# Attention with 192 queries per head: a third of the exponentials moved behind the transpose, with the shift on GpSimd and row sums on TensorE

## Chip, cores, metric

The kernel runs on one core of a Trainium2 chip. The metric is device time in microseconds (us), the median of several executions. Before: 1319.64 us (13 runs, 1319.27 to 1320.28). The record lists all runs named here as fast, that is, none lay more than 1.5% above the fastest of its kernel.

## The reference

```python
B, H, Sq, Sk, D = 16, 32, 192, 1024, 128          # bf16 inputs
def reference(q, k, v):
    scale = q.shape[-1] ** -0.5
    scores = jnp.einsum("bhqd,bhkd->bhqk", q, k) * scale
    p = softmax(scores, axis=-1)
    return jnp.einsum("bhqk,bhkd->bhqd", p, v)
```

## The kernel before

The 512 heads are handled in pairs. A pair has 2 x 192 query rows, which make three **units** of 128 rows: rows 0 to 127 of head a, the same of head b, and the remaining 64 + 64 rows together. So there are 768 units. Sixteen heads, 24 units, form a **group**; the buffers for K, Q and V hold two groups, and there are 32 groups. Per unit:

- TensorE: scores (128x1024), later eight transposes of the probabilities, later the product with V.
- VectorE: a pass that copies the scores out of PSUM, scaled by -1/sqrt(D), and takes the row minimum (which is minus the row maximum); after each third unit, the division by the row sum.
- ScalarE: the exponential, which also accumulates the row sum.
- VectorE and ScalarE by turns: the copy of the transposed probabilities out of PSUM.

```python
# parts of the kernel; "..." and waits not shown are cut
# TensorE
def qk(u):                       # scores; two PSUM buffers
    if u >= 2: pe.wait_ge(s_max, u - 1)
    ...
def tr(u):                       # eight 128x128 transposes
    pe.wait_ge(s_exp, u + 1)
    if u >= 2: wait_evac(u - 2)
    ...
for step in range(NU + 4):
    if step + 1 < NU:       qk(step + 1)
    if 0 <= step - 2 < NU:  tr(step - 2)
    if 0 <= step - 4 < NU:  pv(step - 4)
# VectorE
def rowmax(u):
    dve.tensor_scalar(ss[:, u % NSS, :], s_ps[u % 2][:], -scale, None, ALU.mult, ALU.min,
                      accum_out=nb[:, u % NSS: u % NSS + 1]).then_inc(s_max, 1)
def evac(u):                     # even u here, odd u on ScalarE
    dve.tensor_copy(pt_sb[:, u % NPT], pt_ps[u % 2][:]).then_inc(s_evd, 1)
# ScalarE
def exp(u):
    act.activation(p_sb[:, u % NP, :], ss[:, u % NSS, :], ACT_FN.Exp,
                   bias=nb[:, u % NSS: u % NSS + 1], scale=-1.0,
                   accum_out=rs[:, pr % NRS, O_SLOT[k3]: O_SLOT[k3] + 1]).then_inc(s_exp, 1)
# SyncE: one queue for everything
def loads(g):
    if g >= NS:                  # NS = 2 groups buffered
        e.wait_ge(s_qk, last_u + 1)
        e.wait_ge(s_pv, last_u + 1)
    e.dma_start_transpose(kt[:, s], kf[...])     # K, 4 MB
    e.dma_start_transpose(qt[:, s], qf[...])     # Q
    e.dma_start(vs[:, s], vf[...])               # V, 4 MB
for g in range(NGR):
    if g + NS < NGR: loads(g + NS)
    stores(g)                    # three DMAs, after s_on of the whole group
```

## Time and profile before

| what | value | read from |
|---|---|---|
| median time | 1319.64 us | the runs |
| period of 6 units | 10.01 us, every time | VectorE timeline |
| VectorE busy | 97% | profile page |
| ScalarE busy | 96% | profile page |
| transfers' share | 99.3% of 16 engines' span | queue table |
| instruction fetches | 132 packets | queue table, q8 |

These are lines of the profile page of the kernel before: busy time, the DMA queues (packets, MB, share), the chain that ended last, and groups of instructions (after the first bar: busy us and mean ns of one; after the second: idle time before them).

```profile
PE 1183.6 (90%) x16130; PEld 891.2 (68%) x16384; DVE 1272.9 (97%) x2432; ACT 1259.2 (96%) x1921; POOL 0.7 (0%) x6
...
q1 hardware_dynamic: 790528, 318.78, 99.3%
q8 instruction: 132, 2.16, 0.7%
...
DVE 45%; issue 32%; ACT 16%; PE 3%; SPq 1%; DMA 1%; DVEq 1%; ACTq 0%
...
L259 DVE TENSOR_SCALAR_CACHE_REDUCE ss<-s_ps 128x1024 f32<-128x1024 f32 x768 | 914.9, 1217 | 27.8 <-PE s_ps L175 23.3
L305 ACT ACTIVATE p_sb<-ss,nb 128x1024 bf16<-128x1024 f32 x768 | 877.4, 1144 | 29.9 <-DVE ss L259 21.3
...
L268 DVE COPY pt_sb<-pt_ps 128x1024 bf16<-128x1024 bf16 x384 | 263.4, 686 | 0.9 <-PE pt_ps L210 0.9
...
kt<-in_k_dram SPq DMA_TRANSPOSE x32, 19.4
```

The queue's 99.3% looks like a transfer limit, but the instructions show something else. The row maxima (L259) were idle before their start for 27.8 us in all, of which 23.3 are waits for scores, nearly all for the very first ones. The timeline of VectorE (start, duration, instruction) shows that it never stops:

```profile
603.08 1.22 DVE L259 TENSOR_SCALAR_CACHE_REDUCE ss<-s_ps 128x1024 f32<-128x1024 f32 x1
604.21 0.09 DVE L259 DVE_READ_ACCUMULATOR ss<-s_ps 128x1 f32 x1
604.21 0.17 DVE L277 RECIPROCAL rinv<-rs 128x3 f32<-128x3 f32 x1
604.42 0.56 DVE L279 TENSOR_TENSOR ob<-o_ps,rinv 128x384 bf16<-128x384 f32 x1
604.90 1.22 DVE L259 TENSOR_SCALAR_CACHE_REDUCE ss<-s_ps 128x1024 f32<-128x1024 f32 x1
606.03 0.08 DVE L259 DVE_READ_ACCUMULATOR ss<-s_ps 128x1 f32 x1
606.03 0.69 DVE L268 COPY pt_sb<-pt_ps 128x1024 bf16<-128x1024 bf16 x1
606.64 1.21 DVE L259 TENSOR_SCALAR_CACHE_REDUCE ss<-s_ps 128x1024 f32<-128x1024 f32 x1
```

Read the start-to-start distances: a row maximum holds VectorE 1.14 us, a copy 0.61, a reciprocal 0.21, a division 0.48. Six, three, two and two of them make the 10.0 us of a period. And in stretches of 2 us (columns: stretch, busy time of PE, PEld, DVE, ACT and POOL, granted clock, DMA share, GB/s) the transfers pause at the end of a group; this is one of the groups:

```profile
585.20:587.20 2.00, 1.76 (x22) 1.13 (x21) 2.00 (x4) 2.00 (x4) 0.00 (x0) 1.00 1.12 268
587.20:589.20 2.00, 2.00 (x38) 1.52 (x37) 2.00 (x5) 1.92 (x4) 0.00 (x0) 1.00 0.65 141
589.20:591.20 2.00, 1.75 (x25) 1.43 (x23) 1.97 (x4) 1.98 (x3) 0.00 (x0) 1.00 0.08 17
591.20:593.20 2.00, 1.74 (x30) 1.37 (x30) 2.00 (x6) 1.93 (x5) 0.00 (x0) 1.00 0.00 0
```

The DMA share adds up the times of all packets and comes to more than 1 here (1.12), so these times overlap, and 99.3% over a whole run is not "full". VectorE is the limit of the kernel before, and transfers have time to spare. How much, one group does not tell: the pause shown, 4.9 us between the last packet and the next, is the longest. Over 29 groups of this trace (all but those at start and end) it is 1.8 to 4.9 us, 3.3 on average, so a group's transfers took 36.7 us of its 40.

### The profile page before, as it was taken

To read this page: it belongs to the slowest core of one execution; us is meant where nothing else is said; L and a number is where in the kernel's file an instruction comes from. 1 tells how busy PE (TensorE), PEld (TensorE's weight loads), DVE (VectorE), ACT (ScalarE), POOL (GpSimd) and SP (SyncE) were. 2 spreads that over 40 slices of the span, in tenths; PEclk is the share of its full clock that TensorE was granted. 3 is DMA by queue.
4 is the path that set the end of the run, shared out by engine and by line. 5 is a ranking of instruction groups with operands and counts; after the bars stand their busy time and mean duration, and the time that the engine had idled before them with its cause. 6 is when DMAs were issued, how large, how long until landed. Compare 5 with 4: busy or idle time off the path is not lost.

```text
span 1317.6 us, 40501 instructions
## 1 busy us (share of the span) xinstructions
PE 1183.6 (90%) x16130; PEld 891.2 (68%) x16384; DVE 1272.9 (97%) x2432; ACT 1259.2 (96%) x1921; POOL 0.7 (0%) x6
## 2 busy tenths in 40 slices
PE   2999999999999999999999999999999999999997
PEld 1766767666776666767667676766767667676665
DVE  2899999999999999999999999999999999999997
ACT  2899999999999999999999999999999999999997
POOL 0000000000000000000000000000000000000000
PEclk9999999999999999999999999999999999999999
DMA  9989999999999999899999999999999999999961
GB/s 283 276 193 240 256 253 276 254 215 247 268 242 289 210 252 261 250 258 272 206 261 248 254 279 232 238 259 255 243 278 226 245 258 238 275 271 221 248 200 25
DMA packets 790714, 321.39 MB, mean 244 GB/s; under 512 B 724992, under 2 KB 724992, under 8 KB 790528
## 3 DMA queue, kind: packets, MB, share of 16 engines
q1 hardware_dynamic: 790528, 318.78, 99.3%
q8 instruction: 132, 2.16, 0.7%
q14 instruction: 54, 0.44, 0.1%
HBM read 134.22 MB, written 25.17 MB: 121 GB/s over the span
## 4 chain that ended last, share of the span: by engine, by line
DVE 45%; issue 32%; ACT 16%; PE 3%; SPq 1%; DMA 1%; DVEq 1%; ACTq 0%
DVE ss L259 33%; ACT p_sb L305 15%; DVE pt_sb L268 11%; PE pt_ps L210 1%; SPq L116 1%; DMA vs<-in_v_dram 1%; ACT pt_sb L315 1%; DVE rinv L277 1%; PE s_ps L175 1%; PE o_ps L233 0%; PE o_ps L231 0%; DVEq L258 0%; DVE ob L279 0%; PE s_ps L182 0%; SPq L119 0%
## 5 line engine op out<-in xcount | busy, mean ns | idle before, releaser
L259 DVE TENSOR_SCALAR_CACHE_REDUCE ss<-s_ps 128x1024 f32<-128x1024 f32 x768 | 914.9, 1217 | 27.8 <-PE s_ps L175 23.3
L305 ACT ACTIVATE p_sb<-ss,nb 128x1024 bf16<-128x1024 f32 x768 | 877.4, 1144 | 29.9 <-DVE ss L259 21.3
L210 PEld LDWEIGHTS pt_ps<-ident,p_sb 128*128 128x128 bf16 x6144 | 472.2, 148 | 256.5 <-issue 175.0
L210 PE MATMUL pt_ps<-ident,p_sb 128*128 128x128 bf16 x6144 | 523.6, 228 | 13.0 <-issue 1.3
L315 ACT ACTIVATE pt_sb<-pt_ps 128x1024 bf16<-128x1024 bf16 x384 | 390.9, 1018 | 20.6 <-PE pt_ps L210 9.6
L175 PE MATMUL s_ps<-kt,qt 128*128 128x512 bf16 x770 | 254.3, 386 | 108.6 <-DVE ss L259 59.4
L231 PE MATMUL o_ps<-vs,pt_sb 128*128 128x128 bf16 x4096 | 312.7, 219 | 4.4 <-DMA vs<-in_v_dram 4.4
L268 DVE COPY pt_sb<-pt_ps 128x1024 bf16<-128x1024 bf16 x384 | 263.4, 686 | 0.9 <-PE pt_ps L210 0.9
L231 PEld LDWEIGHTS o_ps<-vs,pt_sb 128*128 128x128 bf16 x4096 | 253.5, 99 | 4.6 <-DMA vs<-in_v_dram 4.6
L175 PEld LDWEIGHTS s_ps<-kt,qt 128*128 128x128 bf16 x1024 | 69.2, 98 | 138.7 <-DVE ss L259 116.8
L233 PE MATMUL o_ps<-vs,pt_sb 128*64 128x128 bf16 x2048 | 162.5, 222 | 0.2 <-ACT pt_sb L315 0.2
L237 PE MATMUL o_ps<-vs,pt_sb 128*64 128x128 bf16 x2048 | 162.5, 222 | 0.2 <-issue 0.2
L182 PE MATMUL s_ps<-kt,qt 128*64 128x512 bf16 x512 | 153.0, 380 | 0.9 <-DVE ss L259 0.5
L188 PE MATMUL s_ps<-kt,qt 128*64 128x512 bf16 x512 | 153.0, 380 | 0.0
L279 DVE TENSOR_TENSOR ob<-o_ps,rinv 128x384 bf16<-128x384 f32 x256 | 142.8, 558 | 8.7
L305 ACT ACTIVATION_READ_ACCUMULATOR p_sb<-ss,nb 128x1 f32 x768 | 145.7, 190 | 0.0
L233 PEld LDWEIGHTS o_ps<-vs,pt_sb 128*64 128x64 bf16 x2048 | 121.0, 109 | 17.8 <-ACT pt_sb L315 0.4
L237 PEld LDWEIGHTS o_ps<-vs,pt_sb 128*64 128x64 bf16 x2048 | 121.0, 109 | 0.0
L259 DVE DVE_READ_ACCUMULATOR ss<-s_ps 128x1 f32 x768 | 64.0, 83 | 0.0
L277 DVE RECIPROCAL rinv<-rs 128x3 f32<-128x3 f32 x256 | 43.3, 169 | 1.6 <-PE o_ps L237 1.6
L182 PEld LDWEIGHTS s_ps<-kt,qt 128*64 128x64 bf16 x512 | 40.7, 109 | 2.2 <-DVE ss L259 1.4
L188 PEld LDWEIGHTS s_ps<-kt,qt 128*64 128x64 bf16 x512 | 40.7, 109 | 0.0
(7 smaller groups left out, 2.2 us busy)
## 6 DMA issues: line engine op xcount, KB each, us to landing
vs<-in_v_dram SPq DMA_DIRECT2D x32, 4096.0 KB, 15.1
out_dram<-ob SPq DMA_DIRECT2D x32, 512.0 KB, 15.9
out_dram<-ob SPq DMA_DIRECT2D x64, 128.0 KB, 4.4
kt<-in_k_dram SPq DMA_TRANSPOSE x32, 19.4
qt<-in_q_dram SPq DMA_TRANSPOSE x32, 6.8
```

The costliest lines, as they stand in the source:

```text
L175: ins = pe.matmul(S[:, cs], qt[:, s, x * SQ: x * SQ + 128], kt[:, s, x * SK + 512 * c: x * SK + 512 * c + 512], start=True, stop=True,)
L182: pe.matmul(S[0:64, cs], qt[:, s, a * SQ + 128: a * SQ + 192], kt[:, s, a * SK + 512 * c: a * SK + 512 * c + 512], start=True, stop=True, ...
L188: ins = pe.matmul(S[64:128, cs], qt[:, s, b * SQ + 128: b * SQ + 192], kt[:, s, b * SK + 512 * c: b * SK + 512 * c + 512], start=True, sto ...
L210: ins = pe.transpose(PT[:, t, :], P[:, t: SK: KT_TILES], ident[:])
L231: ins = pe.matmul(O[:, O_SLOT[k3], :], PTS[:, t, :], vs[:, s, x, t, :], start=first, stop=last)
L233: pe.matmul(O[0:64, O_SLOT[k3], :], PTS[:, t, 0:64], vs[:, s, a, t, :], start=first, stop=last, tile_position=(0, 0),)
L237: ins = pe.matmul(O[64:128, O_SLOT[k3], :], PTS[:, t, 64:128], vs[:, s, b, t, :], start=first, stop=last, tile_position=(0, 64),)
L259: dve.tensor_scalar(ss[:, u % NSS, :], s_ps[u % 2][:], -scale, None, ALU.mult, ALU.min, accum_out=nb[:, u % NSS: u % NSS + 1],).then_inc(s ...
L268: dve.tensor_copy(pt_sb[:, u % NPT], pt_ps[u % 2][:]).then_inc(s_evd, 1)
L279: dve.tensor_tensor(ob[:, so, pg, 0:3, :], o_ps[pr % 2][:, 0:3, :], rinv[:, pr % 2, 0:3].unsqueeze(2).to_broadcast([128, 3, 128]), ALU.mul ...
L305: act.activation(p_sb[:, u % NP, :], ss[:, u % NSS, :], ACT_FN.Exp, bias=nb[:, u % NSS: u % NSS + 1], scale=-1.0, accum_out=rs[:, pr % NRS ...
L315: act.activation(pt_sb[:, u % NPT], pt_ps[u % 2][:], ACT_FN.Copy).then_inc(s_eva, 1)
```

## The change

The intent is to take the PSUM copies off VectorE without overloading ScalarE. Two units of six (route `R_W`) no longer compute the exponential before the transpose. GpSimd subtracts the row minimum (scores are then at most zero after the sign), TensorE transposes the shifted scores, and ScalarE applies the exponential while it empties PSUM: exponential and copy are one instruction. The row sum, which came free with the exponential, is now missing for these units, and TensorE makes it with eight one-column matmuls against ones. The other units keep the exponential in front (`R_EA`, `R_ED`); only one copy of six stays on VectorE. The lags between stages grow, with more buffers; and the K load no longer waits for the value matmuls of the old group.

```diff
+R_EA, R_ED, R_W = 0, 1, 2
+def _attention_kernel(..., LAGS=(2, 4, 5, 7), ROUTES=(R_W, R_EA, R_ED, R_W, R_EA, R_EA)):
 # SyncE, loads(g)
                 if g >= NS:
                     e.wait_ge(s_qk, last_u + 1)
-                    e.wait_ge(s_pv, last_u + 1)
                 e.dma_start_transpose(kt...); e.dma_start_transpose(qt...)
+                if g >= NS:
+                    e.wait_ge(s_pv, last_u + 1)
                 e.dma_start(vs...)
 # GpSimd
+            def shift(u):
+                gp.wait_ge(s_max, u + 1)
+                ...
+                gp.tensor_tensor(x_sb[:, u % NX, :], ss[:, u % NSS, :],
+                    nb[:, u % NSS: u % NSS + 1].to_broadcast([128, SK]), ALU.subtract).then_inc(s_xp, 1)
 # TensorE, pv(u)
+                if with_rs:      # route(u) == R_W; these are first units of a pair
+                    for t in range(KT_TILES):
+                        ins = pe.matmul(O[:, 3, sl: sl + 1], PTS[:, t, :], ones[:, 0:1],
+                                        start=False, stop=t == KT_TILES - 1, skip_group_check=True)
-            for step in range(NU + 4):      # tr two steps, pv four steps after the scores
+            for step in range(NU + L_PV):   # tr four, pv seven
 # VectorE, onorm: one reciprocal more per pair (sums from o_ps and from rs)
 # ScalarE
             def evac(u):
+                if route(u) == R_W:
+                    act.activation(pt_sb[:, u % NPT], pt_ps[u % 2][:], ACT_FN.Exp, scale=-1.0).then_inc(s_eva, 1)
+                else:
                     act.activation(pt_sb[:, u % NPT], pt_ps[u % 2][:], ACT_FN.Copy).then_inc(s_eva, 1)
 (cut: semaphores, counters, waits that follow the routes)
```

More of the change, by code (lines that the diff above doesn't have):

```diff
@@ L9, with _attention_kernel @@
 ALU = mybir.AluOpType
-def _attention_kernel(nc, q, k, v, out, G=16, NS=2):
+R_EA = 0
+R_ED = 1
+R_W = 2
+def _attention_kernel(nc, q, k, v, out, G=16, NS=2, LAGS=(2, 4, 5, 7), ROUTES=(R_W, R_EA, R_ED, R_W, R_EA, R_EA)):
     B, H, SQ, D = q.shape
@@ L21, in _attention_kernel @@
     NU = NGR * UPG
-    NPR = NGR * PPG
     KT_TILES = SK // 128
     scale = float(D) ** -0.5
-    NP = 3
-    NPT = 3
-    NSS = 3
+    L_X, L_TR, L_EV, L_PV = LAGS
+    assert 1 <= L_X < L_TR < L_EV < L_PV
+    NSS = L_X + 2
+    NX = L_TR - L_X + 2
+    NPT = L_PV - L_EV + 2
+    NSO = 2
     NRS = 4
-    NSO = 2
     qf = q.rearrange("b h s d -> (b h) s d")
@@ L35, in _attention_kernel, with route @@
     of = out.rearrange("b h s d -> (b h) s d")
-    def evac_on_dve(u):
-        return u % 2 == 0
-    evac_count = []
-    nd = na = 0
+    def route(u):
+        return ROUTES[u % len(ROUTES)]
+    x_cnt = []
+    ev_cnt = []
+    n_xa = n_xp = n_ea = n_ed = 0
     for u in range(NU):
-        if evac_on_dve(u):
-            nd += 1
-            evac_count.append(nd)
-        else:
-            na += 1
-            evac_count.append(na)
+        r = route(u)
+        if r == R_W:
+            n_xp += 1
+            x_cnt.append(n_xp)
+        else:
+            n_xa += 1
+            x_cnt.append(n_xa)
+        if r == R_ED:
+            n_ed += 1
+            ev_cnt.append(n_ed)
+        else:
+            n_ea += 1
+            ev_cnt.append(n_ea)
     with ExitStack() as es:
@@ L63, in _attention_kernel @@
         ob = sb("ob", [128, NSO, PPG, 4, 128], BF16)
-        p_sb = sb("p_sb", [128, NP, SK], BF16)
-        pt_sb = sb("pt_sb", [128, NPT, KT_TILES, 128], BF16)
         ss = sb("ss", [128, NSS, SK], F32)
         nb = sb("nb", [128, NSS], F32)
+        x_sb = sb("x_sb", [128, NX, SK], BF16)
+        pt_sb = sb("pt_sb", [128, NPT, KT_TILES, 128], BF16)
         rs = sb("rs", [128, NRS, 4], F32)
@@ L81, in _attention_kernel @@
         s_max = sem("s_max")
-        s_exp = sem("s_exp")
+        s_xa = sem("s_xa")
+        s_xp = sem("s_xp")
         s_tr = sem("s_tr")
+        s_eva = sem("s_eva")
         s_evd = sem("s_evd")
-        s_eva = sem("s_eva")
         s_pv = sem("s_pv")
@@ L105, in store_cnt, with wait_x, wait_evac @@
             return 48 * (g // NSO + 1)
+        def wait_x(eng, u):
+            if route(u) == R_W:
+                eng.wait_ge(s_xp, x_cnt[u])
+            else:
+                eng.wait_ge(s_xa, x_cnt[u])
+        def wait_evac(eng, u):
+            if route(u) == R_ED:
+                eng.wait_ge(s_evd, ev_cnt[u])
+            else:
+                eng.wait_ge(s_eva, ev_cnt[u])
         @block.sync
@@ L110, in loads @@
                 s = g % NS
+                last_u = (g - NS + 1) * UPG - 1
+                h0 = g * G
                 if g >= NS:
-                    last_u = (g - NS + 1) * UPG - 1
                     e.wait_ge(s_qk, last_u + 1)
-                    e.wait_ge(s_pv, last_u + 1)
-                h0 = g * G
                 e.dma_start_transpose(
@@ L155, in _ @@
             ).then_inc(s_setup, 1)
+            def shift(u):
+                gp.wait_ge(s_max, u + 1)
+                if u >= NX:
+                    gp.wait_ge(s_tr, u - NX + 1)
+                gp.tensor_tensor(
+                    x_sb[:, u % NX, :], ss[:, u % NSS, :],
+                    nb[:, u % NSS: u % NSS + 1].to_broadcast([128, SK]), ALU.subtract,
+                ).then_inc(s_xp, 1)
+            for u in range(NU):
+                if route(u) == R_W:
+                    shift(u)
         @block.tensor
@@ L194, in qk @@
                 ins.then_inc(s_qk, 1)
-            def wait_evac(u):
-                if evac_on_dve(u):
-                    pe.wait_ge(s_evd, evac_count[u])
-                else:
-                    pe.wait_ge(s_eva, evac_count[u])
             def tr(u):
-                pe.wait_ge(s_exp, u + 1)
+                wait_x(pe, u)
                 if u >= 2:
-                    wait_evac(u - 2)
-                P = p_sb[:, u % NP, :]
+                    wait_evac(pe, u - 2)
+                X = x_sb[:, u % NX, :]
                 PT = pt_ps[u % 2]
@@ L209, in tr @@
                 for t in range(KT_TILES):
-                    ins = pe.transpose(PT[:, t, :], P[:, t: SK: KT_TILES], ident[:])
+                    ins = pe.transpose(PT[:, t, :], X[:, t: SK: KT_TILES], ident[:])
                 ins.then_inc(s_tr, 1)
@@ L217, in pv @@
                     pe.wait_ge(svl[s], load_cnt(g))
-                wait_evac(u)
+                wait_evac(pe, u)
                 if k3 == 0 and pr >= 2:
@@ L222, in pv @@
                 PTS = pt_sb[:, u % NPT]
+                sl = O_SLOT[k3]
                 a = 2 * pg
@@ L225, in pv @@
                 ins = None
+                with_rs = route(u) == R_W
                 for t in range(KT_TILES):
@@ L230, in pv @@
                         x = a if k3 == 0 else b
-                        ins = pe.matmul(O[:, O_SLOT[k3], :], PTS[:, t, :], vs[:, s, x, t, :], start=first, stop=last)
-                    else:
-                        pe.matmul(
-                            O[0:64, O_SLOT[k3], :], PTS[:, t, 0:64], vs[:, s, a, t, :],
-                            start=first, stop=last, tile_position=(0, 0),
-                        )
-                        ins = pe.matmul(
-                            O[64:128, O_SLOT[k3], :], PTS[:, t, 64:128], vs[:, s, b, t, :],
-                            start=first, stop=last, tile_position=(0, 64),
-                        )
+                        ins = pe.matmul(O[:, sl, :], PTS[:, t, :], vs[:, s, x, t, :],
+                                        start=first, stop=last, skip_group_check=True)
+                    else:
+                        pe.matmul(O[0:64, sl, :], PTS[:, t, 0:64], vs[:, s, a, t, :],
+                                  start=first, stop=last, skip_group_check=True, tile_position=(0, 0))
+                        ins = pe.matmul(O[64:128, sl, :], PTS[:, t, 64:128], vs[:, s, b, t, :],
+                                        start=first, stop=last, skip_group_check=True, tile_position=(0, 64))
+                        if with_rs:
+                            pe.matmul(O[0:64, 3, sl: sl + 1], PTS[:, t, 0:64], ones[:, 0:1],
+                                      start=False, stop=last, skip_group_check=True, tile_position=(0, 0))
+                            ins = pe.matmul(O[64:128, 3, sl: sl + 1], PTS[:, t, 64:128], ones[:, 0:1],
+                                            start=False, stop=last, skip_group_check=True, tile_position=(0, 64))
+                if with_rs:
+                    for t in range(KT_TILES):
+                        ins = pe.matmul(O[:, 3, sl: sl + 1], PTS[:, t, :], ones[:, 0:1],
+                                        start=False, stop=t == KT_TILES - 1, skip_group_check=True)
                 ins.then_inc(s_pv, 1)
@@ L244, in _ @@
             qk(0)
-            for step in range(NU + 4):
+            for step in range(NU + L_PV):
                 if step + 1 < NU:
                     qk(step + 1)
-                if 0 <= step - 2 < NU:
-                    tr(step - 2)
-                if 0 <= step - 4 < NU:
-                    pv(step - 4)
+                if 0 <= step - L_TR < NU:
+                    tr(step - L_TR)
+                if 0 <= step - L_PV < NU:
+                    pv(step - L_PV)
         @block.vector
@@ L257, in rowmax @@
                 if u >= NSS:
-                    dve.wait_ge(s_exp, u - NSS + 1)
+                    wait_x(dve, u - NSS)
                 dve.tensor_scalar(
@@ L268, in evac @@
                 dve.tensor_copy(pt_sb[:, u % NPT], pt_ps[u % 2][:]).then_inc(s_evd, 1)
+            ri_total = [0]
             def onorm(pr):
@@ L276, in onorm @@
                     dve.wait_ge(sst[so], store_cnt(g - NSO))
-                dve.reciprocal(rinv[:, pr % 2, 0:3], rs[:, pr % NRS, 0:3]).then_inc(s_ri, 1)
-                dve.wait_ge(s_ri, pr + 1)
+                w_slots = sorted(O_SLOT[k3] for k3 in range(3) if route(3 * pr + k3) == R_W)
+                e_slots = sorted(O_SLOT[k3] for k3 in range(3) if route(3 * pr + k3) != R_W)
+                for slots, src in ((w_slots, o_ps[pr % 2][:, 3, :]), (e_slots, rs[:, pr % NRS, :])):
+                    if not slots:
+                        continue
+                    step_ = slots[1] - slots[0] if len(slots) > 1 else 1
+                    sel = slice(slots[0], slots[-1] + 1, step_)
+                    dve.reciprocal(rinv[:, pr % 2, sel], src[:, sel]).then_inc(s_ri, 1)
+                    ri_total[0] += 1
+                dve.wait_ge(s_ri, ri_total[0])
                 dve.tensor_tensor(
@@ L284, in onorm @@
                 ).then_inc(s_on, 1)
-            for step in range(NU + 8):
+            for step in range(NU + L_PV + 2):
                 if step < NU:
                     rowmax(step)
-                u = step - 3
-                if 0 <= u < NU and evac_on_dve(u):
+                u = step - L_EV
+                if 0 <= u < NU and route(u) == R_ED:
                     evac(u)
-                u = step - 5
+                u = step - L_PV - 1
                 if 0 <= u < NU and u % 3 == 2:
@@ L297, in _, with exp_first @@
         def _(act):
-            def exp(u):
+            def exp_first(u):
+                act.wait_ge(s_max, u + 1)
+                if u >= NX:
+                    act.wait_ge(s_tr, u - NX + 1)
                 pr, k3, g, pg = unit_info(u)
-                act.wait_ge(s_max, u + 1)
-                if u >= NP:
-                    act.wait_ge(s_tr, u - NP + 1)
-                if pr >= NRS and k3 == 0:
+                if pr >= NRS:
                     act.wait_ge(s_on, pr - NRS + 1)
                 act.activation(
-                    p_sb[:, u % NP, :], ss[:, u % NSS, :], ACT_FN.Exp,
+                    x_sb[:, u % NX, :], ss[:, u % NSS, :], ACT_FN.Exp,
                     bias=nb[:, u % NSS: u % NSS + 1], scale=-1.0,
                     accum_out=rs[:, pr % NRS, O_SLOT[k3]: O_SLOT[k3] + 1],
-                ).then_inc(s_exp, 1)
+                ).then_inc(s_xa, 1)
             def evac(u):
@@ L314, in evac @@
                     act.wait_ge(s_pv, u - NPT + 1)
-                act.activation(pt_sb[:, u % NPT], pt_ps[u % 2][:], ACT_FN.Copy).then_inc(s_eva, 1)
-            for step in range(NU + 4):
-                u = step - 3
-                if 0 <= u < NU and not evac_on_dve(u):
+                if route(u) == R_W:
+                    act.activation(pt_sb[:, u % NPT], pt_ps[u % 2][:], ACT_FN.Exp, scale=-1.0).then_inc(s_eva, 1)
+                else:
+                    act.activation(pt_sb[:, u % NPT], pt_ps[u % 2][:], ACT_FN.Copy).then_inc(s_eva, 1)
+            for step in range(NU + L_EV + 1):
+                u = step - L_EV
+                if 0 <= u < NU and route(u) != R_ED:
                     evac(u)
-                if 0 <= step - 1 < NU:
-                    exp(step - 1)
+                u = step - L_X
+                if 0 <= u < NU and route(u) != R_W:
+                    exp_first(u)
 def bass_standalone__mha_softmax__near_ridge_kernel(
```

## The prediction

> **What bounds the kernel now.** The steady state repeats every 6 units (one unit is one 128-row score tile) in 10.01 us, read from the timeline; 128 such periods are 1281 us of the 1317.6 us span, so start and end cost about 37 us. In the timeline VectorE has no gap: start to start, a row maximum (L259) holds it 1.14 us, a copy out of PSUM (L268) 0.61, a reciprocal 0.20, a normalisation 0.48. Six, three, two and two of them are 6.8+1.8+0.4+1.0 = 10.0 us. The page agrees: DVE 97% busy. ScalarE is close behind: exponential with its accumulator read 1.14 us, copy 0.91, so 6x1.14+3x0.91 = 9.5 us. TensorE's 90% is not its limit: where its timeline is dense a unit takes 0.43 (scores) + 0.49 (transposes) + 0.45 (values) = 1.37 us, 8.2 us per period. DMA is 99% in the queue table, but stretches of 2 us show it idle about 5 us of each 40 us group, where SyncE waits for TensorE; a group's transfers need about 35 us, or 8.8 us per period.
>
> **What the change moves, per 6 units.**
> - VectorE: two of three copies leave (-1.22 us); one more reciprocal per pair (2 x ~0.15, estimate from the 0.17 us reciprocal). About 9.1 us.
> - ScalarE: 4 exponentials with accumulator (4.55), 3 plain copies (2.72), 2 exponentials that empty PSUM without accumulator. I take those at 1.0 us: the 0.91 us copy plus about 0.09 for a bias operand (the Trainium skill, "ScalarE: Activation LUTs", What ACT_TABLE_LOAD costs, says each pointer operand adds about 93 ns; 1144 against 1018 ns here is compatible). About 9.3 us.
> - GpSimd: 2 subtractions of 128x1024 f32. No duration in this trace; the Trainium skill, "GPSIMD Engine Reference", Performance versus the Vector engine, gives 4497 ns for 2048 fp32 elements, so an estimate of about 2.3 us each, 4.6 us of 9.3. The transpose comes four steps after the scores, so this should be hidden.
> - TensorE: 16 one-column matmuls with full weight loads for row sums. Estimate 0.056 us each from the pace of the value matmuls, +0.9 us: 9.1 us.
> - DMA: same bytes. K loads are released earlier (they no longer wait for the value matmuls). The limit of about 8.8 us moves near, but stays below.
> - Deeper lags: about 4 us more at start and end.
>
> **On the critical path.** The whole 1.2 us of VectorE copies was on it, but three engines then stand at 9.1 to 9.3 us. ScalarE should bind; I add 0.1 us for waits between engines whose steps are uneven: 9.4 us. 128 x 9.4 + 41 = 1244 us.
>
> **Prediction: 1244 us, 8 in 10 between 1205 and 1290.** Faster by over 2%: 0.84; within 2%: 0.12; slower: 0.04.
>
> **What would show it.** Right: the period near 9.4 us; DVE and ACT both 96 to 99% busy; row maxima gapless or with small waits on the scores; L268 copies down from 384 to 128; GpSimd busy near 45%, seldom named as releaser; the chain of waits shared by ACT and DVE; DMA idle under 3 us per group. Wrong: GpSimd ops of 4 us or more with transposes waiting for them; row-sum matmuls at 0.1 us each, with VectorE waiting for TensorE; VectorE ops lengthened beside GpSimd; the value load waiting, or TensorE waiting for K.
>
> **What would make it wrong.** One-column matmuls costing twice the estimate would put TensorE at 10 us and cancel the gain. A DMA need closer to 37 us would make transfers the bound at 9.3 or above. If the exponential from PSUM costs no more than the copy, 1225 us is possible.

## The result, and the profile after

The kernel after takes 1251.97 us (median of 8 runs, 1249.52 to 1256.14), against 1319.64. Ratios in this document are the mean time of one kernel's fast runs over that of the other's of the same rounds, so they are not quite the ratio of the medians quoted. Here it is 0.9492 (95% interval 0.9479 to 0.9504). The prediction was 1244 us, and 1252 lies in its range. The runs now spread by 0.5%, before by 0.08%. The profiled run is not among the eight and is longer than each of them (1259.49 us, span 1257.8), so averages read from its trace are some 0.6% high.

From the profile page of the kernel after, the lines that answer to those shown of before:

```profile
PE 1174.3 (93%) x18179; PEld 956.4 (76%) x18432; DVE 1149.3 (91%) x2432; ACT 1180.3 (94%) x1665; POOL 486.0 (39%) x262
...
q1 hardware_dynamic: 790528, 318.78, 110.4%
q8 instruction: 148, 2.42, 0.8%
...
PE 88%; DMA 4%; issue 3%; ACT 3%; SPq 1%; DVE 0%; ACTq 0%; DVEq 0%
...
L301 DVE TENSOR_SCALAR_CACHE_REDUCE ss<-s_ps 128x1024 f32<-128x1024 f32 x768 | 910.6, 1220 | 87.9 <-PE s_ps L215 65.4
L188 POOL TENSOR_TENSOR x_sb<-ss,nb 128x1024 bf16<-128x1024 f32 x256 | 485.3, 1896 | 755.6 <-PE pt_ps L244 731.3
...
L370 ACT ACTIVATE pt_sb<-pt_ps 128x1024 bf16<-128x1024 bf16 x384 | 391.6, 1020 | 37.0 <-PE pt_ps L244 35.9
...
L368 ACT ACTIVATE pt_sb<-pt_ps 128x1024 bf16<-128x1024 bf16 x256 | 261.0, 1019 | 8.8 <-PE pt_ps L244 8.8
...
L310 DVE COPY pt_sb<-pt_ps 128x1024 bf16<-128x1024 bf16 x128 | 87.8, 686 | 1.8 <-PE pt_ps L244 1.8
...
kt<-in_k_dram SPq DMA_TRANSPOSE x32, 21.7
```

No engine is at 97% any more, and VectorE has 88 us of waits in front of its row maxima. Taking the start times of the row maxima from the trace, the distance of six units is 9.20 us in the median, but 9.54 on average; a group of 24 units takes 36.8 us when nothing is in the way, and up to 40.4. The first four groups after the start take 35.2 to 37.2 us, and from the ninth on the mean is 38.6. Before, a period was 10.01 us in the median and 10.04 on average.

So two things have to be explained: why the smooth period is 9.20, and what holds groups up. For the first, the timeline of ScalarE in a smooth stretch (accumulator reads left out):

```profile
599.76 1.16 ACT L357 ACTIVATE x_sb<-ss,nb 128x1024 bf16<-128x1024 f32 x1
...
600.90 1.16 ACT L357 ACTIVATE x_sb<-ss,nb 128x1024 bf16<-128x1024 f32 x1
...
602.03 1.03 ACT L368 ACTIVATE pt_sb<-pt_ps 128x1024 bf16<-128x1024 bf16 x1
603.07 1.02 ACT L370 ACTIVATE pt_sb<-pt_ps 128x1024 bf16<-128x1024 bf16 x1
603.99 1.14 ACT L357 ACTIVATE x_sb<-ss,nb 128x1024 bf16<-128x1024 f32 x1
```

An exponential in front still holds ScalarE 1.135 us, a copy 0.905. The exponential that empties PSUM (L368, 1019 ns) costs exactly what the copy (L370, 1020 ns) costs. Four and five of them are 9.07 us; only 0.13 us of a smooth period is slack, mostly at 602.03, where 1.04 us pass.

For the second, the timeline of SyncE's queue, start and time of each issue:

```profile
407.65 18.68 SPq L141 DMA_TRANSPOSE kt<-in_k_dram  x1
426.37 4.68 SPq L144 DMA_TRANSPOSE qt<-in_q_dram  x1
431.10 0.59 SPq L149 DMA_DIRECT2D vs<-in_v_dram  x1
...
445.74 0.72 SPq L164 DMA_DIRECT2D out_dram<-ob  x1
446.50 18.84 SPq L141 DMA_TRANSPOSE kt<-in_k_dram  x1
```

K of the next group is issued right after the last store: the pause of the kernel before is gone, and the queue goes round once in 38.5 us (eight rounds from 407.65 to 716.03). SyncE does not wait for the engines here: from the second such K load on, the scores that it has to wait for were done 11 to 18 us before its issue began. The engines could do a group in 36.8. In the first groups transfers are ahead and the difference is invisible; then the lead is used up, and TensorE starts to wait at group changes. The trace shows for what: in 23 of 30 group changes its first instruction for the new scores starts less than 0.15 us after K and Q, the later of the two, have landed. In the kernel before, K and Q had landed 6.7 to 9.2 us earlier than they were needed.

### The profile page after: what moved, and what is told of

It is laid out like the page before. It is cut to its first block, busy times and chain, and to the rows that moved or that the text cites. A ratio compares the mean times of both kernels' runs of the same rounds, so it can differ in the third digit from the quotient of the medians.

```text
span 1257.8 us, 44565 instructions
## 1 busy us (share of the span) xinstructions
PE 1174.3 (93%) x18179; PEld 956.4 (76%) x18432; DVE 1149.3 (91%) x2432; ACT 1180.3 (94%) x1665; POOL 486.0 (39%) x262
## 3 DMA queue, kind: packets, MB, share of 16 engines
q8 instruction: 148, 2.42, 0.8%
## 4 chain that ended last, share of the span: by engine, by line
PE 88%; DMA 4%; issue 3%; ACT 3%; SPq 1%; DVE 0%; ACTq 0%; DVEq 0%
PE pt_ps L244 32%; PE o_ps L267 18%; PE s_ps L215 16%; PE o_ps L270 11%; PE s_ps L222 8%; DMA vs<-in_v_dram 4%; PE o_ps L281 3%; SPq L141 1%; ACT x_sb L357 1%; ACT pt_sb L370 1%; ACT pt_sb L368 1%; PE o_ps L272 1%; SPq L144 0%; PE s_ps L228 0%; DVE ss L301 0%
## 5 line engine op out<-in xcount | busy, mean ns | idle before, releaser
L188 POOL TENSOR_TENSOR x_sb<-ss,nb 128x1024 bf16<-128x1024 f32 x256 | 485.3, 1896 | 755.6 <-PE pt_ps L244 731.3
L244 PEld LDWEIGHTS pt_ps<-ident,x_sb 128*128 128x128 bf16 x6144 | 480.4, 148 | 217.8 <-issue 143.0
L357 ACT ACTIVATE x_sb<-ss,nb 128x1024 bf16<-128x1024 f32 x512 | 584.9, 1148 | 23.1 <-DVE ss L301 23.1
L244 PE MATMUL pt_ps<-ident,x_sb 128*128 128x128 bf16 x6144 | 524.6, 229 | 1.2 <-ACT pt_sb L368 1.2
L370 ACT ACTIVATE pt_sb<-pt_ps 128x1024 bf16<-128x1024 bf16 x384 | 391.6, 1020 | 37.0 <-PE pt_ps L244 35.9
L368 ACT ACTIVATE pt_sb<-pt_ps 128x1024 bf16<-128x1024 bf16 x256 | 261.0, 1019 | 8.8 <-PE pt_ps L244 8.8
L357 ACT ACTIVATION_READ_ACCUMULATOR x_sb<-ss,nb 128x1 f32 x512 | 101.9, 199 | 0.0
L310 DVE COPY pt_sb<-pt_ps 128x1024 bf16<-128x1024 bf16 x128 | 87.8, 686 | 1.8 <-PE pt_ps L244 1.8
L281 PE MATMUL o_ps<-ones,pt_sb 128*128 128x1 bf16 x2048 | 87.5, 164 | 0.0
L281 PEld LDWEIGHTS o_ps<-ones,pt_sb 128*128 128x128 bf16 x2048 | 78.2, 96 | 0.0
```

The costliest lines, as they stand in the source:

```text
L188: gp.tensor_tensor(x_sb[:, u % NX, :], ss[:, u % NSS, :], nb[:, u % NSS: u % NSS + 1].to_broadcast([128, SK]), ALU.subtract,).then_inc(s_x ...
L244: ins = pe.transpose(PT[:, t, :], X[:, t: SK: KT_TILES], ident[:])
L281: ins = pe.matmul(O[:, 3, sl: sl + 1], PTS[:, t, :], ones[:, 0:1], start=False, stop=t == KT_TILES - 1, skip_group_check=True)
L357: act.activation(x_sb[:, u % NX, :], ss[:, u % NSS, :], ACT_FN.Exp, bias=nb[:, u % NSS: u % NSS + 1], scale=-1.0, accum_out=rs[:, pr % NRS ...
L368: act.activation(pt_sb[:, u % NPT], pt_ps[u % 2][:], ACT_FN.Exp, scale=-1.0).then_inc(s_eva, 1)
L370: act.activation(pt_sb[:, u % NPT], pt_ps[u % 2][:], ACT_FN.Copy).then_inc(s_eva, 1)
```

## The experiments

The theory, A: the engines alone would run at 9.20 us a period, and the transfers, at 38.5 us a group, set the time. The rival, B: the engines hold each other up at group changes, whatever the transfers do. A leads to a second question, because I had counted only 35 us of transfers in a group: where do the other 3.5 us come from?

### a1_no_v and b1_no_v: V loaded only twice

Wrong, with the same instructions on the compute engines.

```diff
-                if g >= NS:
-                    e.wait_ge(s_pv, last_u + 1)
-                e.dma_start(vs[:, s], ...).then_inc(svl[s], 16)
+                if g < NS:
+                    e.dma_start(vs[:, s], ...).then_inc(svl[s], 16)
-                    pe.wait_ge(svl[s], load_cnt(g))
+                    pe.wait_ge(svl[s], 16)
```

> The kernel after, with V loaded for the first two groups only (the output is wrong on purpose; instructions and waits of the engines are the same). Theory A (the engines alone would repeat every 9.20 us, and the transfers, at about 38.5 us a group, hold groups back): all periods 9.20 us, 22.7 + 127.8 x 9.20 + 16 = about 1215 us. Rival B (the engines hold each other up at group changes, whatever the transfers do): stays at 1250 us.

> The kernel before with the same cut (wrong output on purpose). Its transfers were said to fit in the 40 us of a group: unchanged, 1318 to 1320 us. If transfers cost the kernel before anything, it falls below 1315.

Measured: 1216.17 us for the kernel after without V (1214.7 to 1217.85; ratio to the kernel before 0.922), 1319.5 us for the kernel before without V. Nearly all groups of a1 take 36.7 to 36.9 us. So transfers cost the kernel after 36 us and the kernel before nothing. A holds, B falls. The granted clock is 0.998 instead of 0.988, but that looks like a result of the waits, not a rival cause: the trace of the kernel after grants half the clock for 3.4 us (once 6.8) at seven group changes, each at the end of a group of 39.2 us or more, after TensorE had waited; the trace of a1 does so only at its end.

### d1_dma_only: the transfers alone

```diff
-    (all work of TensorE, VectorE, ScalarE; the subtraction on GpSimd)
 # loads(g), for g >= NS
-                    e.wait_ge(s_qk, last_u + 1)
+                    e.wait_ge(sxk[s], load_cnt(g - NS)); e.wait_ge(sxq[s], load_cnt(g - NS))
-                    e.wait_ge(s_pv, last_u + 1)
+                    e.wait_ge(svl[s], load_cnt(g - NS))
 # stores(g): the output tile is set to zero once
-                e.wait_ge(s_on, (g + 1) * PPG)
+                e.wait_ge(s_setup, 3)
```

> The same loads and stores in the same order from the same queue, without the compute (the output is zeros, wrong on purpose). Theory A in its plain form (the DMA engines need about 38 us a group whatever else runs): 32 x 38 = about 1220 us. If the transfers alone need only the 35 us a group that I predicted: about 1120 us; then it is their order and waits, not their volume, that holds the kernel after. Far below 1100: transfers are slowed by the compute beside them.

Measured: 1067.94 us. The transfers by themselves go round in 33.2 us. So the plain form of A is wrong: the volume does not need 38.5 us; something slows the transfers while the engines work.

The trace of the kernel after names a suspect. In the stretch from 612 to 616 us, cut into 40 slices of 0.1 us, the K transposes run at 290 GB/s, then stop for about 1.2 us, in a stretch in which one packet of another queue, q8 (instructions), ran:

```profile
DMA  9999999999999900000000000089999999999999
GB/s 287 300 289 287 294 289 289 289 289 435 271 271 269 161 0 0 0 0 5 8 8 10 10 8 10 13 182 289 289 287 289 292 287 289 292 289 294 294 289 289
...
q8 instruction: 1, 0.02, 1.5%
```

These packets are the engines' own program. The Trainium skill, "Runtime: NRT & Kernel Launch", Instruction fetch mechanics, says that an engine's instruction memory is refilled in blocks of 16 KiB by a DMA queue that the sequencer drives. This trace agrees: 148 packets make 2.42 MB, 16.4 KB each, and the 44,565 instructions of the kernel after are mostly TensorE's. I counted the packets of the transposes in the 4 us after each of the 75 fetches that met them at full speed: in the median, packets worth 1.4 us are missing. That gives theory C: each instruction fetch halts the transposing transfers for about 1.4 us. Its rival, D: transfers are slowed by the compute engines' use of the on-chip memory, whatever is fetched.

### d2_dma_fetch and d3_dma_traffic: one suspect each

```diff
 # d2: d1 plus
+            for i in range(18200):      # one weight load and one matmul each, constant data
+                pe.matmul(o_ps[0][:, 0:2, 0:80], ones[:], ob[:, 0, 0, 0:2, 0:80], start=True, stop=True)
 # d3: d1 plus, each with two output buffers and its semaphore
+            for i in range(260):  gp.tensor_tensor(x_sb[...], ss[:, 2, :], nb[...], ALU.subtract)
+            for i in range(980):  dve.tensor_scalar(ss[:, i % 2, :], s_ps[0][:], -scale, ..., accum_out=...)
+            for i in range(980):  act.activation(x_sb[:, i % 2, :], ss[:, 3, :], ACT_FN.Exp, ..., accum_out=...)
```

> The transfers alone, beside a TensorE that only runs 18,200 idle matmuls (as many instructions as the kernel after gives it, on constant data, output zeros and wrong on purpose). Theory C (each 16 KB fetch of instructions holds the transposing transfers up for about 1.4 us; some 145 fetches): 1068 + 145 x (1.0 to 1.6) = 1210 to 1300 us by the stalls if every one hits a transpose, about 1180 us if half do. Rival D (the transfers are slowed by the compute engines' use of the on-chip memory): 1068 to 1080 us, as this TensorE reads next to nothing.

> The transfers alone, beside VectorE, ScalarE and GpSimd running the tile operations of the kernel after (980 row maxima, 980 exponentials, 260 subtractions of 128x1024, on constant data), with a tenth of the instructions. Theory C: 1068 plus about 18 fetches x 1.4 = 1070 to 1095 us. Rival D: near 1200 us.

Measured: 1271.92 us and 1135.7 us. I had set both expectations for the whole time, and that was a mistake of design: in both runs the added engine work lasts longer than the transfers (TensorE is busy 99% of d2, VectorE 99% of d3), so the total says nothing. The transfers must be read by themselves. These are the issues of K for the fourth and the last group in SyncE's queue, for d1, d2 and d3:

```profile
92.28 15.18 SPq L142 DMA_TRANSPOSE kt<-in_k_dram  x1
...
1022.96 15.27 SPq L142 DMA_TRANSPOSE kt<-in_k_dram  x1
```

```profile
103.80 17.95 SPq L142 DMA_TRANSPOSE kt<-in_k_dram  x1
...
1142.11 16.93 SPq L142 DMA_TRANSPOSE kt<-in_k_dram  x1
```

```profile
94.59 15.04 SPq L142 DMA_TRANSPOSE kt<-in_k_dram  x1
...
1027.67 15.31 SPq L142 DMA_TRANSPOSE kt<-in_k_dram  x1
```

Over 28 groups, that is 33.2 us a group alone, 37.1 beside 142 fetches of instructions, and 33.3 beside full VectorE, ScalarE and (for the first 40% of the run) GpSimd work with few instructions. (The page of d3 shows no q8 packets; its 4,445 instructions came with 34 packets of 8 KB on another instruction queue, q14.) C holds, and D falls for the engines of d3. In d2 TensorE's use of the memory grew together with its fetches, and no run separates the two, but the traces do. Between stalls the transfers are as fast in all of them: the median slice of 0.1 us that has packets of 256 bytes (transposes and stores) has 112 of them in d1, d2, d3 and the kernel after alike. Stalls of such packets of 1 to 3 us, with full speed before and after, number none in d1, one in d3, 62 in d2 and 67 in the kernel after; a q8 packet runs in, or within 1.5 us before, 58 of those 62 and all 67.

The remaining 1.4 us between 37.1 and the 38.5 of the kernel after were not settled by a run. Fetches come more often there (148 in 1257.8 us are 4.5 in a round; 142 in 1270.1 us are 4.1 in one of d2), and the q14 queue has 53 packets against 2 in d2; transposes pause beside some of these too, mostly for less than 1 us (near 609.4 us, for about 0.4).

### a2_wait_back: the old place of the wait

```diff
                     e.wait_ge(s_qk, last_u + 1)
+                    e.wait_ge(s_pv, last_u + 1)
                 e.dma_start_transpose(kt...)
 ...
-                if g >= NS:
-                    e.wait_ge(s_pv, last_u + 1)
                 e.dma_start(vs...)
```

> The kernel after with the wait for the value matmuls put back in front of the K load, as the kernel before has it. If transfers are the limit and the earlier start of K matters: slower than 1252, by up to 11 us a group where they are late (seven units of lag x 1.55 us), at most 1400 us. If SyncE reaches that wait only after it has been met, because its queue runs late by itself: unchanged within 5 us.

Measured: 1254.47 us (1252.7 to 1256.54; ratio to before 0.9507, interval 0.9493 to 0.9521, which overlaps that of the kernel after). This part of the change is worth nothing that can be measured here: SyncE's queue is late by itself.

### r2_old_routes and r3_no_gpsimd: one part of the change alone

```diff
-ROUTES=(R_W, R_EA, R_ED, R_W, R_EA, R_EA)
+ROUTES=(R_ED, R_EA)                                   # r2: split as before, long lags kept
+ROUTES=(R_EA, R_EA, R_ED, R_EA, R_EA, R_EA)           # r3: copies moved, no GpSimd
```

> The kernel after with its longer lags and earlier K loads, but the work split as in the kernel before (copies out of PSUM by turns on VectorE and ScalarE, no GpSimd, no row-sum matmuls). Theory: the gain is the moved work alone, so VectorE is full again at 10.0 us a period: 128 x 10.0 + 41 = about 1321 us. If lags or the earlier loads carried part of the gain: below 1310.

> The kernel after with copies moved off VectorE, but every exponential at ScalarE before the transpose (no GpSimd, no row sums). ScalarE then has six exponentials with accumulator and five copies: 6 x 1.135 + 5 x 0.905 = 11.3 us a period, 128 x 11.3 + 41 = about 1490 us, much slower than before: unloading VectorE alone is a loss.

Measured: 1315.43 us and 1486.84 us. In r2 the period is 10.01 us again. It is 4 us faster than the kernel before: its first group takes 37.4 us instead of 44.0, and the time after the last row maximum grows from 12.1 to 14.5. All but these 4 us of the gain need the moved work. In r3 the period is 11.34 us with ScalarE busy 98%: emptying VectorE alone makes the kernel 12.7% slower (ratio 1.1269). The fused exponential is what pays for the copies that come to ScalarE.

### r1_one_rowsum: fewer instructions in the real kernel

Wrong: one of eight row-sum matmuls is left.

```diff
-                    for t in range(KT_TILES):
-                        ins = pe.matmul(O[:, 3, sl: sl + 1], PTS[:, t, :], ones[:, 0:1], ...)
+                    ins = pe.matmul(O[:, 3, sl: sl + 1], PTS[:, 0, :], ones[:, 0:1], ...)
```

> The kernel after with one of the eight row-sum matmuls left per block (wrong output on purpose). 1,792 matmuls and as many weight loads less, 229 KB of instructions, 14 fetches of 16 KB. Theory C (fetches hold the transposes up, and transfers set the time): 14 x 1.4 = about 20 us less, 1228 to 1240 us. If transfers set the time but fetches do not matter: unchanged within 5 us. If TensorE's time mattered, the smooth period would fall below 9.20 us; I expect it to stay.

Measured: 1230.2 us (1228.6 to 1231.61), with 134 fetches instead of 148. From the ninth group on, a group takes 37.5 us instead of 38.6. The time fits theory C, but the run does not isolate it, because the smooth period fell too, against my expectation, from 9.20 to 9.09 us. That is close to the 9.07 us of ScalarE's own work. So in smooth stretches the row-sum matmuls on TensorE had cost 0.1 us a period beyond ScalarE's limit.

### p1_v_pool, p2_v_act and p3_v_pool_late: V on a queue of its own

The load of V does not have to stand in the queue of the transposes and stores.

```diff
 # SyncE: V for the first two groups only
-                if g >= NS:
-                    e.wait_ge(s_pv, last_u + 1)
-                e.dma_start(vs...)
+                if g < NS:
+                    e.dma_start(vs...)
 # GpSimd (p1, p3), after the subtraction of unit u; in p2 the same on ScalarE, at the start of step u
+            def load_v(u):
+                g = u // UPG + 1
+                if u % UPG != 9 or not NS <= g < NGR:      # p3: 15 instead of 9
+                    return
+                gp.wait_ge(s_pv, (g - NS + 1) * UPG)
+                gp.dma_start(vs[:, g % NS], vf[...]).then_inc(svp[g % NS], 16)
 (cut: TensorE waits for V on svp from the third group on; p2 keeps the semaphore svl)
```

> The kernel after with the V loads (from the third group on) issued by GpSimd on a queue of its own, once the group two before is through, so that they can run beside the transposes of K and Q. If the transfer engines as a whole are the limit (no free time in them): 1250 us, unchanged. If the limit is one queue that stands still during a stall of the transposes, V fills the holes: towards the 1216 us of the run without V, 1216 to 1235. If GpSimd's issue of a load takes over 4 us, row blocks will wait for its subtractions and it gets slower.

> The same, issued by ScalarE. ScalarE sets the 9.20 us period, so its issue (0.59 us on SyncE) is paid in full: 36.8 + 0.6 = 37.4 us a group, 1235 us, if V then no longer waits; 1250 us or more if the transfer engines as a whole are the limit.

> As p1_v_pool, but V is issued six units (9 us) later in a group, when the transposes of K and Q should have landed. If the two groups of p1 that lost 9 and 11 us lost them because V ran beside the transposes: all groups 36.8 us, 1216 to 1222 us. If they lost them for another reason: near 1235 again. If V now comes too late: value matmuls wait for it, over 1240.

Measured: p1 1234.95 us (1230.15 to 1241.69), p2 1298.52 us (1293.53 to 1300.36), p3 1219.83 us (1217.75 to 1220.67; ratio to before 0.9243). All three are correct. In p1 most groups take 36.7 us, but two take 46.0 and 47.5; around these, the issue of Q lasts 20.6 and 15.5 us instead of 4: V got in among the transposes. The trace shows how: the two queues take turns, about one packet each. From 85 to 90 us of p1, 75 to 95 packets of Q (256 bytes each) go through in a microsecond beside about as many of V (4 KB each), where 1,134 packets of the transposes go through without V (77 to 78 us). In the other 28 groups V ran almost only beside the stores, and K and Q had landed 9 us or more before they were needed. p2 has the same trouble in most groups, and my expectation for it was wrong by 60 us: the issue on ScalarE took only 0.38 us, but the loads of K and Q landed late. Their lines in the page of p2:

```profile
kt<-in_k_dram SPq DMA_TRANSPOSE x32, 29.3
qt<-in_q_dram SPq DMA_TRANSPOSE x32, 18.8
```

p3 starts V six units later and is the version that beats both kernels. SyncE's queue in p3 has its pause back in 18 of 30 groups, mostly about 5 us between the last store and the next K (V is under way then):

```profile
426.81 23.81 SPq L142 DMA_TRANSPOSE kt<-in_k_dram  x1
450.66 4.12 SPq L145 DMA_TRANSPOSE qt<-in_q_dram  x1
...
458.30 0.63 SPq L164 DMA_DIRECT2D out_dram<-ob  x1
463.61 23.75 SPq L142 DMA_TRANSPOSE kt<-in_k_dram  x1
```

Groups take 36.9 us on average (36.8 in most), and the time is 4 us above the run without V. The fetches are as many as before (148): p3 does not remove the stalls. It takes V out of the line behind them, and K and Q land over 1.2 us before they are needed in every group. V now runs beside the stores (the two small ones take 14.5 us to land instead of 4.4), and the issue of the next K lasts longer, 23.8 us instead of 18.7. How much of this comes from V using the stalls, and how much from V running beside the stores, was not separated.

## Why the prediction was right, and where it was wrong

The time was right to 8 us, but two errors of opposite sign stand behind that, so its closeness was partly luck: a smooth period of 9.20 instead of 9.4 us takes 26 us off 128 periods, and the transfers, which were not to matter, put 36 us back.

- **VectorE was the limit, and its copies were on the critical path**: right. Copies fell from 384 to 128, the period from 10.01 to 9.20 us; r2 and r3 show that the moved work, and only together with the fused exponential, makes the gain (all but some 4 us of it).
- **"ScalarE should bind", at 9.3 us a period**: in smooth stretches nearly so; its own work is 9.07. The term that was mis-sized is the exponential that empties PSUM: 0.905 us like the copy, not 1.0. I had allowed 0.09 us for a bias operand; the call in the kernel names none, and 1019 against 1020 ns shows no extra cost.
- **VectorE at 9.1 us**: about 8.9. The second reciprocal starts 0.08 us after the first (601.09 and 601.17 in the trace) and adds about 0.06 us, not 0.15.
- **GpSimd at 2.3 us a subtraction, hidden**: 1.90 us, and hidden. 731 of the 756 us that GpSimd was idle went on waiting for a buffer that a transpose frees.
- **TensorE, +0.9 us for the row sums**: too high. Eight of them take 0.34 us from first start to last end, with a single one at 0.16, so about 0.025 us each instead of 0.056, some 0.4 us a period. Even so, r1 shows that these matmuls cost 0.1 us of the smooth period, which a sum of 8.2 + 0.4 does not explain. The 8.2 us added up dense stretches alone; what TensorE's waits between them add was not measured.
- **Waits of 0.1 us a period between uneven steps**: 0.13 us, by the sum above.
- **"The limit of about 8.8 us moves near, but stays below"**: this step failed. A group's transfers took 38.5 us, 9.6 us a period, and set the time from about the ninth group on. The mean period is therefore 9.54, not 9.20, and 36 us are given back (1252 against 1216 without V). Two things went wrong. The 35 us fit the one group shown above, with the longest of 29 pauses; the mean of the same trace is 36.7 us, 9.2 a period, no less than the smooth period of the new kernel. And I had read it as a fixed need. It is 33.2 us of work plus stalls that depend on how many instructions the engines fetch; the added row sums raised the fetches from 132 to 148. The text did name this case ("a DMA need closer to 37 us") among what would make it wrong, without a cause.
- **Deeper lags, "about 4 us more at start and end"**: the end grew by 3.9 us (12.1 to 16.0 after the last row maximum), but the first group shrank from 44.0 us to 35.2; r2, which has the lags and the earlier loads without the moved work, is 4 us faster than before. Which of the two shortened the first group was not separated.
- **Signs named beforehand**: DVE and ACT at 96 to 99% came out as 91 and 94%; the chain of waits shows TensorE with 88%, not ScalarE and VectorE; the transfers' pause is gone instead of under 3 us. In the run without V, where transfers do not matter, VectorE is at 95% and ScalarE at 97%. The chain names TensorE in that run too, since TensorE is occupied almost always when three engines stand level; by itself it does not show which of them sets the period.

## What to carry to other kernels

When the engine that limits a kernel is relieved, count again everything that had slack, and take the transfers' need from a run of the transfers alone and one beside the real number of instructions, not from their busy share, nor from one group of a trace. A fully unrolled program is itself a transfer load, and a DMA that transposes suffers from it: every matmul added brought two instructions to fetch. When a queue carries loads and stores in a fixed order and is late by itself, moving one large load to another queue, timed after the transposes, gained 2.6% here (1251.97 to 1219.83 us), and timed during Q's transposes (p2) it lost.

## What the Trainium skill lacked or had wrong

- "Runtime: NRT & Kernel Launch", Instruction fetch mechanics, calls the cost of crossing a 16 KiB boundary mostly hidden. For the engine that may be so; the transfers pay. Beside 142 fetches, the same transfers took 37.1 us a group instead of 33.2, and a fetch that met a transpose took about 1.4 us of it.
- "DMA: Bandwidth & Descriptors", DMA Transpose (X-bar), does not say that transposes stand still beside an instruction fetch. In the kernel after they did so for 1 to 3 us 67 times, each time beside one of its 148 fetches.
- "DMA: Bandwidth & Descriptors", Issuing engines are not separate DMA queues, says that issuing from several engines only saves the issue time. Moving the V loads from SyncE to GpSimd took the kernel from 1251.97 to 1219.83 us (p3), 32 us less, where the 0.59 us of an issue in each of 30 groups would be 18; what changed is the loads that stand behind one another.
- "GPSIMD Engine Reference", Performance versus the Vector engine, gives 4497 ns for an fp32 `tensor_tensor` of 2048 elements. Half of that, as an estimate for 1024, is 2.25 us; the subtraction of 128x1024 f32 with a broadcast operand and bf16 output took 1.90 us.
- No page says that the share of DMA packets' time can exceed that of the engines: the transfers alone read 114.1% in the queue table of d1.
